# A new issue list for a fused attention and double feed-forward kernel: order, engine letters and buffer places

## The chip, the cores and the metric

The kernel runs on 1 core of one Trainium2 chip. The metric is device time in microseconds (us) of one execution, lower is better. The names of the engines are those of the profile: PE (TensorE, matmuls), PEld (TensorE's weight loads, which overlap PE), DVE (VectorE), ACT (ScalarE), POOL (GpSimd) and SP (SyncE, which here issues every DMA).

## The reference

Four batches of eight heads (576 positions, 64 wide) go through causal attention that is mixed with a read from a memory matrix, then through two feed-forward layers (512 to 2048 to 512) with different non-linearities.

```python
scores = where(causal, -1e9, scale * q @ k.T);  a = softmax(scores);  local = a @ v
q_p = where(q > 0, q, exp(q) - 1) + 1
mem_out = (q_p @ M_prev) / (q_p @ z_prev + 1e-6)
g = 1 / (1 + exp(-beta))
x = g * mem_out + (1 - g) * local          # heads side by side: 2304 x 512
h = x @ w_in;   g1 = where(h >= 1, h, where(h <= -1, 0, (h + 1)**2 / 4));  y = g1 @ w_out
h = y @ w_in2;  g2 = maximum(h, 0) + alpha * minimum(h, 0);                return g2 @ w_out2
```

## The kernel before

Every value that goes into a large matmul is split into a float16 head and a float16 rest, and each product is made of three float16 matmuls (head by head, head by rest, rest by head). The work is written section by section: `prepare` (sums and scales of a batch), `attend` (attention of a pair of heads), `Weights.groups` and `SumsIn.group` (weights arrive as float32 words and are scaled and split), `up1` and `down1` (first feed-forward layer, for each batch `b` and each of two halves of 288 tokens), `ffn2` (second layer, by a scheme with seven products in place of eight).

No section calls an engine. The class `Plan` (lines 86 to 136) records each operation with its number, 0 to 4286 in the order in which the sections write them. Many operations are recorded in more than one way (`either`, line 105): a scaling copy can be made by ACT, DVE or POOL (`copy`, line 225), the rest of a split by DVE in one instruction or by POOL in two (`rest`, line 243), a difference by DVE or POOL (`combine`, line 240), bits of a weight by DVE or ACT (`rest_of`, line 309). A group of matmuls under `plan.one()` is one operation, for example the 12 matmuls of 288 columns that give one block of `up1`.

Two tables written out by hand decide the rest. `ISSUE` (line 1259) lists the 4287 numbers in the order of issue, with a letter `a`, `v` or `g` (ACT, DVE, POOL) behind a number that has a choice; each engine, and SP with its DMAs, then takes its own instructions in that order. `PLACES` (line 1176) says for every tile of a name which of the buffers of this name it takes, as a string of digits. A tile that takes a buffer over waits until the tile before it there has been used for the last time. The instructions are all recorded in line 135, `fn(*args, **kw)`, so the profile shows L135 everywhere and is read by tiles.

Some names: `f` is the PSUM buffer (two of them, each for two blocks) of `up1`, `down1` and the last products; `d` and `u` are the steps of the first non-linearity (DVE clamps `f` into `d`, ACT squares it, DVE makes `u` out of `f` and `d`, which frees `f`); `g` holds the split result, `wt` and `wb` pass the weights through, `wa` holds w_in, `p` and `tt` are the softmax weights and their transpose, `s` and `px` are the smaller PSUM buffers (two each).

```python
    def run(self):
        engines = dict(a="act", v="dve", g="pool")
        order = ISSUE.split()
        ...
            for t in order:
                op = self.ops[int(t.rstrip("avg"))]
                eng = engines[t[-1]] if op.key else next(iter(op.ways))
                for fn, args, kw in op.ways[eng]:
                    fn(*args, **kw)
```

Of the kernel before, what the change touches and what calls it, by code (L numbers as in the profile page):

```python
# [1156 lines left out]
def _order():  # L1157
# [11 lines left out]
    for b in range(B):  # L1169
# [15 lines left out]
    "sb.qn": (640, "132040130124213041320423120431324014203114210420143042314034021324101340023123011243"),  # L1185
# [4 lines left out]
        "1010010110111001011110010110010101110010011010011010010101011010101010100101101010100101101010011001"  # L1190
        "1010100100011110010101101010101001101010011010010110100101010110010101011001011010100110101001011000"
        "011001110011000000100011101001100111110011101001110100001110011100",
    ),
    "tiny.arm": (1, "100010110"),
    "tiny.ard": (8, "0101"),
    "tiny.m3": (3, "0101"),
    "tiny.p2m1": (1, "01000101111001001001010101010110000000010101"),
    "tiny.p2e1": (1, "01001111000110011010001011010000010011011001"),
# [3 lines left out]
    "tiny.p2i3": (3, "0110"),  # L1202
# [4 lines left out]
    "sb.wt": (1024, "100101000011001101101101101101101101101100100110"),  # L1207
    "tiny.wmg": (1, "1001110001010101"),
    "tiny.ws": (1, "10011100001100111010101010100110"),
    "sb.x": (1152, "23011001011002130210321023103120321"),  # L1210
    "sb.vf": (1152, "1021021221021021021021012010"),
    "sb.qk": (1152, "101001011010101101010101"),
    "ps.px": (512, "10100101001011000111000001001100010011011001011100101101010001010101101010100011"),
    "tiny.mxt": (4, "32010121032313022310102301320113022303120112230231300122310231302103"),
    "tiny.sm": (4, "32010121032010322013132031320113022303120102231230312011302130021320"),
    "sb.e": (1152, "021201002121200102120121021020120120122001112020122001211022020101210212012"),
    "sb.p": (1280, "0010011001100110100101110001100011100011101010010101100010110100011001101010"),
    "sb.tt": (1280, "010101011101100010010110011001110001100010101001010110100111100001101000101010010101"),
    "ps.f": (
        1024,  # L1220
        "1010011001101011010010111010000101011010100100010011100101100101001100010110101001011110100110011010"
        "1001100101001011011010011101010010000010111011001100",
    ),
    "tiny.inv1": (8, "01010101"),
# [10 lines left out]
    "sb.g": (1152, "02133021420412043021410321034021324013240132410324"),  # L1235
    "sb.u": (
        576,
        "0101010110110001000111011010110001001011011100101010100100001111100101010101001001101011110000110110"
        "0101001110010011110100111001",
    ),  # L1240
    "sb.d": (576, "010010111011000111000110010100111001010101101010010101100000111101010101010110101010011010010101"),
    "tiny.wmx": (1, "0011001110100110"),
    "tiny.ysc": (4, "010101010101"),
    "sb.y": (288, "1110100100101001111010010101101010110011011011111010110010100010"),
# [8 lines left out]
    "tiny.p2s1": (1, "01001111"),  # L1253
    "tiny.p2i1": (1, "01000111"),
# [8 lines left out]
205 156 204 233 87v 160 231 840 33 161 169 170v 162 312 46 239a 173v 214 47 206 207 163 48 20 208a 164 209g 172 50  # L1263
210v 49 827 223v 15 211 1311 165 215 313 167a 174 129v 217 168v 18 212a 213 104 85 236v 238 216 315 235 240 120 218
237 495 171 241 219 220 122 314 21 221g 121 242 841 175 222v 462 842 243 123 166 107 244 124 245 246 224 463 125 248g
109 843 111 335a 108 249v 133 110 225a 19 320v 226 332v 268 331 126 134 266 128g 127a 135 136 142g 529 333 130 137 526
112 251v 113 852 51 115a 114g 52 334 116g 53 138 117 54 336 55 118a 197g 56 131a 139 59 119 57 188 58 141v 140a 132 60
189 349 190 191 317v 269 265 192 61 143 337 271 464 62 193 194 63 270 195g 273 278v 338 196g 272 502v 198 144a 274 176
65 64 304g 339 199a 145 340 341 342 275 344v 277a 200 276a 348 467a 279 66 591 345v 227a 836 148a 146a 828 177 316 346
247 350 319 318 560 853 178 321 834 179 322 180 147v 347 182g 149v 352 351 267 280a 181 323 229v 354 183v 353 829 324  # L1270
830 250 355 295 325 253 252 326 835 327 255 329g 328 860 356 256 297 296 357v 299 330v 257 481a 298 258 466 282 300
259 228v 470a 301 468 303a 302g 260 343 494 283 577a 262 261 359g 284 305 230v 469 263v 285 471 286 363 306a 291g 465
287 264v 631 472 307 365 501 288 358v 290v 498 360 289v 473 499v 292 361a 364 367 500 362 366 503 496 484a 393 474 837
376 475 394 368 372v 476 293v 504 478g 844 281 369 377 370a 378 505 371g 294 379 479v 380 373 628 385g 374v 483 480
485 548a 381 477 497 506 395 482 630 382 507 384a 508 383g 396 310v 397 486 308v 510g 386 309v 375 387a 402 511v 831
388 513v 512 832 403 398 594 515 514 487 389a 68 527 488 531a 390v 593 489 509 629 407 490 399 516v 492a 517 493v 406
518 558 592 401 491 530 405 519 404 456 408 534a 532 533 409 520 455 535 521 536 559 523 522 410 524g 632 666 457 391a
537 563a 421 411g 668 538 458 642g 604v 525v 833 420 412g 459 562 913 539 565 541 413 540 422 460g 845 564 423 414
461g 528 566a 424 542a 567 442 415 561 543g 311v 416 441 568 417 392v 434 418a 443 419v 444 435 425v 545a 445 426g 547
544 428 436 549 437 569 546 427 861 446g 570 438 550 447g 571 633 572 429 580a 448 574g 430 634 635 636 575v 595 637  # L1280
638 449 573 576 639 596 641g 431 598 640g 597 579 643 578 599 646 450 620g 644a 854 600 601 648 451 590 603g 647 581
667 649 439a 602g 400 582 645 651 708 440g 650 653 605 432v 652 583 551 658g 584 855 552 654 862 608 655 452 657g 606a
707 610 656g 661 609 856 453v 659 662a 857 611 660a 858 613 669 663 863 612 670 615 454g 859 722 705 614 553 607 706
723 664a 718g 724 864 616 725 617 665v 618a 619g 726 433g 621 727 728 623 585 622v 709 729 734g 865 846 624a 704 730
711 866 625 1085 731 710 713 554 712 732g 671 867 733a 714 586 715 626a 735 672 717g 847 737 673 716g 848 736v 684
680g 738a 849 719 675 685 850 674 686 627v 687 720a 676 739 696g 677 555 689 679a 678g 688 691 588g 851 681 690 910
868 721 869 682a 870 692 871 693 873 589v 874 694a 683 556a 875 697 876 872 695a 877 764 878 890 698a 879 880 887 888
881 882 889 883 699 891 885 892 914g 765 700a 893 587 884 915g 740v 911a 701 912v 995 743 702a 894 905 895 1086a 900
886 703v 2574 901 744 903 941 766 952g 942 931g 742 944 896 943 906g 767 945 953v 907v 996a 741v 1329 916 557v 768 745
1087v 750 919 1000 1750 923 918 908 920 899 1330 997v 746 922 1093 917 937a 946 947 1003 948v 1312 960 949v 747 909  # L1290
924 950v 806 749 1001g 961 921 1339 925 951v 963 932g 926 807 748 954 927g 929v 933g 962 1004g 898 964 751 938g 1005v
1002v 752 928v 808 975 934v 809 1751 930v 753 935v 965 810 936g 966 977 811a 792 902 939 1752 976 754 1340 969g 978
1341 904 955 979 1090 793 981 999 970v 756 1094g 980 998 982 812v 800 971g 967a 983 794 972g 1021a 968g 799 1753 795
940 1265 1027g 796 973 1095g 1006 801 757 1009 802 1010 1007 1028g 1008 1013 758 803 1022g 1014 1089 958a 1342 1011
1012 759 1754 797a 959v 1015 1759 1091v 798g 984 1016 1017a 1019a 771 985a 989v 987v 1023a 990v 760 1018v 804a 1347
# [207 lines left out]
```

## Time and profile before

| | us |
|---|---|
| median of 3 runs | 967.76 (967.29 to 969.53) |
| profiled execution | 971.3 |
| its span, first to last instruction | 969.5 |
| PE busy | 899.2 (93%), 8043 matmuls |
| PEld busy | 679.8 (70%) |
| DVE busy | 732.9 (76%), 1905 instructions |
| ACT busy | 520.1 (54%), 1109 instructions |
| POOL busy | 393.6 (41%), 487 instructions |
| DMA | 144.5 MB, 53.7% of the engines' span |

The profile page gives the span in 40 slices of some 24 us, each with a digit for the busy tenths. The view by stretches gives the same in us for stretches of one's choice, the view of waits says which instruction ended the idle time of an engine, and the timeline lists instructions in order of time. "Idle before" an instruction is the time in which its engine did nothing ahead of it.

### The profile page before, as it was taken

The numbers are of one execution on the slowest core, as the hardware profiler recorded it, in microseconds if no ns is written. First come the engines' busy times: TensorE is split into PE (matmuls) and PEld (weight loads), VectorE is DVE, ScalarE is ACT, GpSimd is POOL, SyncE is SP. The second block draws the span as 40 slices with busy tenths as digits, with TensorE's granted clock in tenths as the row PEclk, the third lists the DMA queues.
The fourth block names the chain that finished last, engine by engine and source line by source line (L and its number), as shares of the span: only waits on it lengthen the run. The fifth ranks groups of instructions, "written<-read, shape, count | busy, mean of one in ns | idle before, by whom it ended". The sixth has DMA issues, their size and how long they took to land. (4 is left out here: it accounts for less than half of the span.)

```text
span 969.5 us, 21105 instructions
## 1 busy us (share of the span) xinstructions
PE 899.2 (93%) x8043; PEld 679.8 (70%) x8043; DVE 732.9 (76%) x1905; ACT 520.1 (54%) x1109; POOL 393.6 (41%) x487
## 2 busy tenths in 40 slices
PE   1567999999999998998999999989999999999998
PEld 1345667777777766766677778767777777777776
DVE  5988898898888989979887688899767767464400
ACT  6988895687766757657765344466312212121100
POOL 3222673754647546466446252364322114121210
PEclk9968999999999999999999999999999999999999
DMA  8965334689848688368786436556433432331000
GB/s 284 346 212 193 99 121 145 121 182 183 191 113 172 126 168 178 123 178 195 166 188 191 130 134 220 191 174 221 136 126 105 154 93 81 99 101 46 25 25 26
DMA packets 157190, 144.52 MB, mean 149 GB/s; under 512 B 100000, under 2 KB 119968, under 8 KB 157088
## 3 DMA queue, kind: packets, MB, share of 16 engines
q1 hardware_dynamic: 157088, 143.17, 53.7%
q8 instruction: 63, 1.03, 0.5%
q14 instruction: 39, 0.32, 0.1%
HBM read 99.63 MB, written 16.78 MB: 120 GB/s over the span
## 5 line engine op out<-in xcount | busy, mean ns | idle before, releaser
L135 PEld LDWEIGHTS <-wb 128*128 128x128 f16 x3072 | 297.6, 98 | 86.2 <-issue 9.3
L135 PEld LDWEIGHTS <-wa 128*128 128x128 f16 x2880 | 279.6, 98 | 90.1 <-issue 17.9
L135 PE MATMUL f<-g,wb 128*128 128x288 f16 x2160 | 283.5, 287 | 3.2 <-DVE u L135 1.5
L135 PE MATMUL f<-x,wa 128*128 128x288 f16 x1536 | 201.1, 288 | 7.3 <-DVE u L135 6.5
L135 ACT ACTIVATE e<-e,mxt 128x192 f32<-128x192 f32 (+4 forms) x160 | 88.1, 551 | 32.2 <-DVE mxt L135 27.8
L135 PE MATMUL px<-x,wa 128*128 128x288 f16 x672 | 97.4, 286 | 2.0 <-DVE qn L135 2.0
L135 PE MATMUL s<-x,wa 128*128 128x288 f16 x672 | 97.8, 287 | 1.1 <-DVE qn L135 1.1
L135 ACT ACTIVATE y<-f,ysc 128x288 f32<-128x288 f32 x64 | 31.6, 496 | 119.1 <-PE f L135 101.0
L135 ACT ACTIVATE d<-d,bu,su 128x576 f32<-128x576 f32 x64 | 55.3, 864 | 52.8 <-DVE d L135 52.4
L135 POOL TENSOR_TENSOR g<-u,g 128x576 f16<-128x576 f32 x46 | 62.7, 1365 | 31.1 <-ACT g L135 14.1
L135 PE MATMUL s<-qk 64*128 64x288 f16 (+9 forms) x528 | 65.5, 322 | 5.8 <-DVE mxt L135 3.8
L135 DVE SCALAR_TENSOR_TENSOR qn<-qn,al 128x576 f32<-128x576 f32 x64 | 53.8, 852 | 13.5 <-ACT qn L135 13.1
L135 DVE TENSOR_SCALAR d<-f,lim 128x576 f32<-128x576 f32 x64 | 55.8, 872 | 10.1 <-PE f L135 9.7
L135 PE MATMUL px<-tt,vf 128*64 128x128 f16 (+3 forms) x1320 | 58.0, 236 | 4.0 <-ACT tt L135 2.6
L135 POOL TENSOR_SCALAR p<-e,sm 128x448 f16<-128x448 f32 (+9 forms) x52 | 31.4, 609 | 71.2 <-DVE sm L135 44.3
L135 DVE SCALAR_TENSOR_TENSOR u<-f,sd,d 128x576 f32<-128x576 f32 x64 | 52.1, 814 | 10.5 <-ACT d L135 9.2
L135 DVE CUSTOM_DVE_ANT_0 e<-s,mask,qs 128x192 f32<-128x192 f32 (+4 forms) x120 | 55.1, 482 | 4.8 <-PE s L135 4.6
L135 DVE SCALAR_TENSOR_TENSOR p<-e,sm,p 128x320 f16<-128x320 f32 (+4 forms) x89 | 51.9, 599 | 4.3 <-POOL p L135 2.0
L135 PE MATMUL f<-vf,wb 128*128 128x288 f16 x384 | 52.3, 286 | 0.0
L135 ACT ACTIVATE p<-e,sm 128x448 f16<-128x448 f32 (+8 forms) x80 | 43.1, 563 | 13.5 <-DVE sm L135 8.5
L135 PE MATMUL f<-e,wb 128*128 128x288 f16 x336 | 45.7, 286 | 0.0
L135 POOL TENSOR_TENSOR g<-qn,g 128x288 f16<-128x288 f32 x32 | 26.7, 845 | 42.7 <-ACT g L135 16.6
(249 smaller groups left out, 1398.9 us busy)
## 6 DMA issues: line engine op xcount, KB each, us to landing
wa<-w2i_d SPq DMA_DIRECT2D x32, 768.0 KB, 4.8
tmp<-in_qk SPq DMA_DIRECT2D x36, 288.0 KB, 3.3
wb<-in_w1i SPq DMA_DIRECT2D x16, 512.0 KB, 8.0
wt<-in_w2i SPq DMA_DIRECT2D x16, 512.0 KB, 4.2
w2i_d<-tmp SPq DMA_DIRECT2D x24, 256.0 KB, 2.6
x<-in_w1o SPq DMA_DIRECT2D x11, 512.0 KB, 3.9
qn<-in_qn SPq DMA_DIRECT2D x16, 320.0 KB, 4.0
tmp<-in_vc SPq DMA_DIRECT2D x16, 320.0 KB, 4.1
```

The costliest lines, as they stand in the source:

```text
L135: fn(*args, **kw)
```

## The change

Only the two tables change. The 4287 operations, their sections and their arithmetic stay. In `ISSUE` 4152 of the 4287 numbers stand in another place, most of them by few places. PE's 834 groups of matmuls keep their sequence but for small swaps: of the 558 groups that run before 675 us none moves by more than 11 places. SP's 426 DMAs move by 4.5 places on average. Of the 1388 operations with a choice of engine, 550 get another letter:

| from \ to | DVE | ACT | POOL |
|---|---|---|---|
| DVE | | 86 | 141 |
| ACT | 84 | | 65 |
| POOL | 95 | 79 | |

In `PLACES` the digits of most names change; the number and the size of the buffers do not. The diff, cut to its beginning and its kinds:

```diff
     "sb.tmp": (
         640,
-        "1110102011102220020000112122001212111000010211220021101220110021012102001210200102122112002010212121"
-        "0000201112021211202211022010121021021021",
+        "1200001210221210022020210212001220010202121012022100220202012120112011000212000112220021000212010121"
+        "0000210010200212022121101021102210102102",
     ),
...
-    "sb.wa": (2048, "012303213201320103210310132001231230"),
-    "sb.wb": (2048, "102313203120"),
+    "sb.wa": (2048, "012303123103120302310132101320313012"),
+    "sb.wb": (2048, "103212301230"),
...
 ISSUE = """
-1 72 2 1304 0 40 5 3 13 4 6 22 69 34 91 1305 1310 92v 1306 71 1307 93 41 1308 42 70 7 8 23 9 10 43 24 28 1309 11 44
-74a 151 73 35 25 234 36 75 89a 26 45 838 88 12 76 187 90 37 29 185 94 27 150 38 77a 95 184 30 78 16 39 79 153 31 839
-80 96 32 105 254a 97 152 81 98 201 100 99 82 158v 101a 83 186 84 106 86a 102v 232 17 203 202 157 155v 14 154 159 103
...
+1 22 3 5 34 0 2 1304 40 13 6 23 72 28 24 1305 70 1306 35 25 36 1307 71 26 1308 41 42 69 37 91 7 1310 27 38 187 29 153
+92a 43 77a 8 39 44 150 1309 88 9 30 93 76 151 89v 74a 90 73 78 14 94 75 45 79 231 95 31 80 152 1311 155a 10 96 32 173a
+81 97 201 82 16 98 158a 83 100 11 4 84 99 12 33 86g 101a 232 202 203 15 87v 827 204 236a 103 102v 157 104 154 184 159
...
```

Numbers 69 to 72 are the loads of the first group of w_in's words, 94 and 79 are ACT's squares of that group (its scale comes from them), 95 and 80 the matmuls that sum these squares.

## Rows read from the trace of the kernel before

**Rows 1.** The page: span, busy time of each engine, and PE's 40 slices.

```profile
span 969.5 us, 21105 instructions
...
PE 899.2 (93%) x8043; PEld 679.8 (70%) x8043; DVE 732.9 (76%) x1905; ACT 520.1 (54%) x1109; POOL 393.6 (41%) x487
...
PE   1567999999999998998999999989999999999998
```

**Rows 2.** Stretches: length, busy PE, PEld, DVE, ACT, POOL; clock, DMA share, GB/s.

```profile
0.00:125.00 125.00, 79.22 (x481) 53.12 (x482) 99.70 (x318) 102.49 (x210) 42.76 (x55) 0.88 0.68 226
125.00:350.00 225.00, 221.75 (x2298) 161.89 (x2298) 199.93 (x614) 161.01 (x384) 129.54 (x160) 1.00 0.68 149
350.00:510.00 160.00, 147.95 (x1580) 107.67 (x1577) 143.08 (x414) 110.98 (x245) 85.43 (x115) 1.00 0.74 173
510.00:640.00 130.00, 128.17 (x1083) 101.71 (x1081) 102.43 (x207) 60.38 (x100) 53.06 (x57) 1.00 0.52 170
640.00:675.00 35.00, 30.92 (x238) 23.50 (x237) 33.66 (x56) 24.09 (x46) 21.32 (x18) 0.95 0.61 207
675.00:969.50 294.50, 291.17 (x2376) 231.94 (x2374) 154.06 (x301) 61.19 (x129) 61.51 (x83) 1.00 0.27 87
```

**Rows 3.** Waits of PE, 0 to 125 us: total, times, longest.

```profile
PE s L135 <- ACT wa L135: 24.3, 4, 12.9
```

**Rows 4.** Waits of PE, 350 to 510 us.

```profile
PE f L135 <- DVE u L135: 5.4, 5, 1.8
PE s L135 <- DVE mxt L135: 2.7, 6, 1.8
...
PE px L135 <- DMA tt<-p: 0.7, 1, 0.7
```

**Rows 5.** Timeline, 371 to 377 us, of DVE, POOL and PE: start, us, instruction.

```profile
372.35 1.30 POOL L135 TENSOR_TENSOR p<-e,p 128x576 f16<-128x576 f32 x1
372.43 1.77 DVE L135 SCALAR_TENSOR_TENSOR wt<-wt,wt 128x512 int32<-128x512 int32 x1
...
374.86 0.81 DVE L135 SCALAR_TENSOR_TENSOR u<-f,sd,d 128x576 f32<-128x576 f32 x1
...
375.73 1.51 PE L135 MATMUL f<-x,wa 128*128 128x288 f16 x11 [1.75 <-DVE u L135]
```

**Rows 6.** Groups by shape: busy us and mean ns of one, then idle before.

```profile
L135 POOL TENSOR_TENSOR g<-u,g 128x576 f16<-128x576 f32 x46 | 62.7, 1365 | 31.1 <-ACT g L135 14.1 <-DVE p2s L135 7.6 <-DVE g L135 4.8
...
L135 DVE TENSOR_TENSOR g<-u,g 128x576 f16<-128x576 f32 x18 | 14.6, 817 | 0.8 <-ACT g L135 0.7
...
L135 ACT ACTIVATE u<-s,sa 128x288 f32<-128x288 f32 x17 | 8.4, 494 | 4.2 <-PE s L135 4.2
```

**Rows 7.** Instructions by tile (wt, then d): duration min/median/max in ns.

```profile
L135 DVE SCALAR_TENSOR_TENSOR wt<-wt,wt x16: 680/684/1771, 238.7 to 561.9; 128x512 int32<-128x512 int32 x16
L135 DVE SCALAR_TENSOR_TENSOR wb<-wt,ws,wb x13: 1273/1284/2426, 79.5 to 685.9; 128x1024 f16<-128x1024 f32 x13
...
L135 DVE TENSOR_SCALAR d<-f,lim x64: 847/874/879, 92.7 to 582.2; 128x576 f32<-128x576 f32 x64
```

**Rows 8.** Timelines: SP's loads and ACT's squares at the start.

```profile
0.74 0.39 SPq L135 DMA_DIRECT2D wb<-in_w1i  x1
...
3.54 0.43 SPq L135 DMA_DIRECT2D wb<-in_w1i  x1
...
8.49 0.65 SPq L135 DMA_DIRECT2D qn<-in_qn  x1
...
15.55 0.75 ACT L135 ACTIVATE wb<-wb,half 128x512 int32<-128x512 uint16 x1
...
17.95 1.04 ACT L135 ACTIVATE wa<-wt 128x1024 bf16<-128x1024 f32 x1
```

**Rows 9.** Timeline at the end, and up1's matmuls of the first 125 us by duration.

```profile
L135 PE MATMUL f<-x,wa x192: 283/286/448, 88.5 to 119.4; 128*128 128x288 f16 x192
...
966.26 0.50 ACT L135 ACTIVATE y<-f,ysc 128x288 f32<-128x288 f32 x1 [5.38 <-PE f L135]
```

More of the change, by code (lines that the diff above doesn't have):

```diff
@@ L1210 @@
[L1210 to L1216, printed above, removed]
@@ L1217 @@
-    "sb.p": (1280, "0010011001100110100101110001100011100011101010010101100010110100011001101010"),
-    "sb.tt": (1280, "010101011101100010010110011001110001100010101001010110100111100001101000101010010101"),
+    "tiny.ws": (1, "01011100001100111010101010101010"),
+    "sb.x": (1152, "32011010001013021302130213012031023"),
+    "sb.vf": (1152, "0101120212012012012012021020"),
+    "sb.qk": (1152, "101001011010010010101010"),
+    "ps.px": (512, "10101101110100110111000000101111100011010001011010100010010101101011101110101011"),
@@ L1219 @@
+    "tiny.mxt": (4, "32010121032313022310102301320113022303121002231230311022301230312013"),
+    "tiny.sm": (4, "32010121032312033210103201230112033202131013320321203100213321103201"),
+    "sb.e": (1152, "021201002112200102120121020121021021002112220101200112022102121010201202102"),
+    "sb.p": (1280, "1001010110010100100101110001100011101001101010010101010010100111100101001001"),
+    "sb.tt": (1280, "100101001110010101101001100101010010001110010110101010011100011110110001101001101010"),
     "ps.f": (
@@ L1220 @@
         1024,
[L1221 to L1222 removed]
+        "1001010001011011010010110011000110001010110111000011100110001100011100010110101011001001010101100101"
+        "0110101010110100010101010101101001111100001101101101",
     ),
[L1224 removed]
+    "tiny.inv1": (8, "01010110"),
     "tiny.bd": (1, "01010101"),
@@ L1252 @@
     "tiny.ym1": (1, "0101"),
-    "tiny.p2s1": (1, "01001111"),
-    "tiny.p2i1": (1, "01000111"),
+    "tiny.p2s1": (1, "01001110"),
+    "tiny.p2i1": (1, "01001010"),
     "tiny.amx": (1, "0"),
@@ L1265 @@
[L1265 to L1274, printed above, removed]
@@ new lines @@
+1212 1213 1214 1131v 1215 1155 1326 1134 1316 1274 1216 1157 1327 1156 1217 1220a 1158 1218v 1083a 1272 1275 1222g
+1160 1317 1219g 1159 1162 1328 1186 1161 1223g 1221v 1120 1313 1187 1163 1290 1819 1164 1224 1189 1165a 1167g 1190
+1188 1169a 1084v 1193 1170g 1135 1271 1194 1168v 1291 1140 1191 1166v 1192 1280 1195 1142 1171 1196 1207g 1201a 1197v
+1276 1205a 1141 1198g 1199a 1203a 1200v 1136a 1202g 1208v 1143 1225 1204v 1206v 1144 1137v 1230 1209 1138a 1281 1232
+1145 1234 1146 1231 1151g 1282 1147v 1233 1152g 1292 1314 769 1148g 1331 1139v 1283 1277 1149a 1278 1279 1235 1241g
@@ new lines @@
+1559 1739 1713v 1562a 1560g 1712v 1930 1563v 1715 1955 1561g 1931 2423 1923 897 1716 1742a 1925 1717 1963 2422 1924
+1740a 1745v 1566 1743v 1718 1741g 2430 2424 1933 2425 2429 1719 2426 1956 1720 2436 2427g 1721 2431 2611a 1957 2432
+2437 2428v 1964 1958 2433 1953 2438 1724a 2415 1960 2434a 1746 1965 1722a 1725v 2416 2439 1966 1959 2610 2440 1567
+1961 2417 2435g 2441a 2401 1726a 1967 2418 1727g 2612 2402 1984 2419 2613 1723v 2420a 2614 1985 1728 2403 1934 2394
+1986 2615 2404 1987 2616 1989 2617 1568a 1990 2619 2395 2618 1991 1988 1992 2026 2620g 2442g 2621g 2622g 2421g 2627a
@@ new lines @@
+2921 3163a 2973 2810a 2962 2922 3173 2974a 2811g 2923 2963 2924 3157g 2812 2935 2964 3199 2912 3143 2965 2925v 2934
+2975v 2926g 2966 3175 2936 3225 2948 2571 3155v 2937 3164v 3010 2967a 2949 2938 3016 3176 2939v 3251 2950 3200 3202
+2940g 2919 3112 2951 3226 2813g 2952 3113 2814v 2953a 3158v 3015 3179 2954v 3167a 2976 3174 3171g 3144 3105 3145 3146
+3147 3148 3149 3150 3151 3017 3106 3180a 2968v 3027 3107 2980 3172v 3169a 3203v 3108 2981 2572 2982 3170v 3201 2978
+3109 2986 3177v 3114 3111 3110 3011 3178 2815 3204 2987 3181 2988 2989 2990 2991 3183 3168v 3207 2992v 3119 3182v
@@ new lines @@
+3590 3534v 3536v 3591 3531v 3506 3413 3483v 3501 3393 3504v 3502g 3505v 3089g 3594 3542 3547 3597 3394 3598v 3503g
+3545 3509g 3414 3546a 3548 3553 3395 3415 3482v 3554g 3555g 3549 3510g 3566 3550 3556g 3601 3103v 3567a 3551 3507g
+3599 3552v 3615 3508g 3616 3396 3558 3484g 3399 3559v 3397 3602 3560g 3600 3557g 3565 3603 3568 3605 3400 3604a 3824
+3823 3564 3618 3726 3569 3619a 3416 3617 3570v 3608v 3606g 3607g 3571 3620 3609g 3644 3572a 3438 3561a 3405 3645a 3575
+3573 3406 3574 3579 3407 3610 3576 3611a 3582a 3612g 3621 3408 3622v 3727v 3583v 3401 3409 3613v 3580v 3614v 3410
@@ new lines @@
+3949a 3951g 3908a 4020v 3698 3821g 3950v 3952g 3909 3699 3910v 3700 3913 3911 4023a 3914 4034 3701 4025g 3912 3915
+3917 4060 4021g 3916a 4109 4027a 3702 4008 3692 3822g 4110 3920v 4028v 4059 4022v 3693 3918v 4009 4061v 3919v 4063
+4035v 4062 4033 3922 3694 4029v 3925a 4064a 3923v 4024v 4037 3926v 3695 3924v 3709 3696 3893v 4084 4036 4026v 3710
+4030v 3921v 4039 4067 4040a 4038a 4065 3711 4066v 4068 4073 4086 4069 4076g 4087a 4041 4070 4043 4042 4071 4089 4072v
+4044 3712 4090v 4047 4085 3713 4045 3714 4088 4161 4078 4093 4046a 4213 4010 4091 4079a 4048a 3977 4092v 4162 4094
@@ new lines @@
+4052 4115 4099 4055a 3959 4050a 4053g 4102a 4056v 4116a 4054g 4112 4080v 4051g 4095 4113v 4100g 4111 4081v 4077g 3960
+4114 4082g 4103g 4096 4117 4097 4118a 4074a 3961 4098v 4135 4104 4119 4107v 4105g 4049v 4121 4106g 3978 4108v 4101g
+4120 4125 4163 4128v 4138 4129v 4122 3979 4126v 4127v 3962 4137 3963 4123 3964 3980 4124a 4188 4130 3953 4131a 4133v
+3981 4134v 4139a 4132g 3982 4136 4164 4187 4167 3708 4165v 3954 4166 4168a 4140 4169 3971 4170a 3955 4173 3956 4174
+4141 3957 4143 4142a 4145 4175 4171 4176a 3989 4172 3972 3973 3974 4193 3975 4144a 3965 3976 4194v 4146 4151 3966
@@ new lines @@
+4152g 4153v 3967 4177 4180v 4182 4147 4183a 3990 4184v 4148 4075v 3968 3991 3969 4178a 3970 4179g 4149 4185g 3992
+4186g 4150v 4156 4190 3993 4216 3994 4191a 4214 4219 4217v 3983 4220a 4154a 4155g 4197 4215 4189 3984 4192 3995 3996
+3997 4195 3998 4196v 4198 4203 3985 3999 4159a 4204v 4000 4218 4206v 4223 4207g 4199 4160g 3986 4200 4157g 4201 3987
+4221 3988 4202a 3958 4208 4251 4211v 4209g 4212v 4252 4158g 4222v 4224 4210g 4225 4205g 4257 4226 4229 4227 4232v
+4230g 4253 4231g 4228a 4234 4233g 4258 4235g 4237g 4236g 4259 4238g 4181g 4254 4260 4255 4281 4261 4262 4282 4283 4284
@@ L1446 @@
+4239 4285 4286 4240 4269 4270 4271 4272 4241 4273 4274 4242 4245 4243 4244 4275 4276 4246 4247 4248 4277 4249 4250
+4278 4263 4279 4280 4256 4264 4265 4266 4267 4268
 """
```

350 lines of the change are left out of this document (161 added, 189 removed).

## The prediction

> **What bounds the kernel now.** I read the page first, then the stretches, then the waits of PE in the stretches where it is idle. On the page [rows 1] PE is busy for 899.2 of 969.5 us, and its slices show where it is not: in the first four, then a little in the middle (two digits of 8). The stretches [rows 2] give that in us. From 0 to 125 us PE is idle for 125 - 79.2 = 45.8 us; from 125 to 350 for 3.2; from 350 to 510 for 12.1; from 510 to 640 for 1.8; from 640 to 675 for 4.1; and from 675 to the end for 3.3. So PE sets the time from about 125 us on, and there are 45.8 us to win or lose at the start and 3.2 + 12.1 + 1.8 + 4.1 = 21.2 us in the middle. The last 3.3 us are no stall: the last copy out of PSUM starts at 966.26, behind PE's last matmul [rows 9], and its store follows. Behind 675 us nothing can be won, since 2376 matmuls in 291.2 us are one in 122.5 ns at a clock of 1.00, 2.4 GHz, and 288 columns at 2.4 GHz take 120.
>
> What holds PE at the start: it waits 24.3 us for ACT's `wa` (the squares from which a weight group gets its scale), more than half of its idle time there [rows 3]. ACT is busy for 102.5 of these 125 us, DVE for 99.7 [rows 2]; both are nearly full, and the chains run through both.
>
> What holds PE in the middle: of 350 to 510 us the two largest waits are for DVE, 5.4 us for `u` and 2.7 for `mxt` [rows 4]. DVE is busy for 143.1 of 160 us there, and for 199.9 of 225 before [rows 2]. One such wait stands in the timeline [rows 5]: DVE is at a weight instruction of 1.77 us, then `u` starts at 374.86, and only then PE, idle for 1.75 us, gets its `f` buffer back. So DVE, in its own queue, runs late by a few us, and PE has only two `f` buffers to bridge that.
>
> **The change, part by part.** Nothing is added to PE, and its sequence hardly moves, so its work stays as it is. What can change is when its inputs come.
>
> *Letters.* 227 operations leave DVE and 179 come to it. I counted them by the stretch in which the trace runs them, and priced each by its own duration on the engine it leaves and the mean of its shape on the engine it goes to. Two kinds stand in [rows 6]: the rest `g<-u,g` takes 0.82 us on DVE and 1.37 on POOL, a copy `u<-s,sa` 0.49 on ACT. For DVE this gives:
> 0 to 125 us: 26 leave, 17 come, -3.2 us;
> 125 to 350: 60 and 42, -9.4;
> 350 to 510: 35 and 26, -5.4;
> 510 to 675: 33 and 34, +1.7;
> later: 73 and 60, -6.2 (PE waits for nothing there, so worth nothing).
> To 510 us that is 36 instructions fewer, 18.0 us, half a us each. POOL gets +2.4, +17.9, -0.6, -1.3 and +13.5 us in the same stretches, ACT +2.4, -0.6, +8.9, +1.2 and -4.4.
>
> *Order.* It works the same way. Ahead of the `u` of [rows 5] DVE has 836 operations in the old list and 805 in the new one, while PE's place is the same but for a few groups. So the relief is ahead of the stalls, not behind them.
>
> *What POOL's time costs DVE.* The same timeline shows why DVE was late just there [rows 5]: the `wt` instruction took 1.77 us beside a POOL instruction of 1.30, and its median is 0.68 [rows 7]. Instructions of DVE that read PSUM do not show this: `d<-f,lim` takes 0.847 to 0.879, 64 times [rows 7]. How much more the added POOL time costs, the trace does not show directly. One bound is 0. The other is that each added us of POOL stops DVE for one us: 2.4 + 17.9 - 0.6 = 19.7 us by 510, more than the 18.0 of relief. From rows: `wt<-wt,wt` has a mean of 0.865 (16 take 13.8 us) against a minimum of 0.680, `g<-u,g` on DVE 0.817; stretches of 10 to 25% where both inputs come from SBUF. POOL is busy for 215 of the 385 us from 125 to 510 [rows 2], and 17.3 more is 8%; 8% of a stretch of some 20% on half of DVE's 343 us is under 3 us. I take 2.
>
> The Trainium skill, "SBUF — State Buffer", section "Who interferes with whom", says that a DVE instruction with two SBUF inputs and a GpSimd instruction that reads SBUF take an exclusive lock, and the one that comes second is blocked for the whole instruction. The trace agrees [rows 5] (1.77 is near 0.68 plus most of 1.30). By that rule alone the price would lie at its upper bound and the time at 971 us; that is the first rival.
>
> *The middle, summed.* DVE is relieved by 18 - 2 = 16 us by 510. PE can win back no more than it lost. Of the 12.1 us of 350 to 510 I take two thirds, -8: most waits for DVE go, those like the 0.7 us for a DMA [rows 4] stay. Of the 3.2 before, a third, -1. Of 1.8 + 4.1 behind, a third, -2: the wait near 650 us is also a chain of its own, and once PE is earlier there DVE has only some us more in hand. What is late next is POOL, with slower rests (1.37 for 0.82) that `down1` and the attention wait for; but it is busy half of the time, and ACT with +8.9 from 350 to 510, at 111 of 160 us. For such new stalls I put +1, between 0 and +6 (half of the gain). Sum of the middle: -10, between -21 and +2.
>
> *The start.* ACT has 14 instructions ahead of the first square (17.95 us) and 16 in the new list; at 0.75 us [rows 8] the first sum of squares comes 1.5 us later. On SP, the four loads of this first group stand in places 1, 7, 9 and 10 of the queue, now 7, 9, 10 and 11: the last one is issued at 8.49 rather than before it, and the first at 3.54, the seventh issue, rather than at 0.74 [rows 8]. Against that ACT gets other loads to work on first. Over 125 us ACT gets +2.4 us and DVE -3.2. I take +2 for the start, between -3 (DVE's relief is felt in full) and +7 (the late weights and ACT's extra time add up, and some of up1's first matmuls fall to the lower clock). The trace shows a granted clock of 0.88 over these 125 us, and up1's matmuls at 0.286 and, at the lower level, 0.448 us [rows 9].
>
> *Sum*: -10 + 2 = -8 us on the profiled 971.3 (span 969.5 and 1.8 around it), 963. That execution is 3.5 us above the median of the runs, so against the median 967.76 the forecast is 959.8 us.
>
> **The rivals.**
> *POOL takes it back (slower).* Place: DVE between 125 and 510 us. Price: with a share r of the added 19.7 us blocking DVE, the relief is 18.0 - 19.7 r. The middle's gain of 10 shrinks in proportion, 10 x (18.0 - 19.7 r) / 16, and the start's +2 outweighs it from r = 0.75 on. At r = 1 the stalls grow by 1 and the start adds 2: 971. For it speaks the blocked `wt` [rows 5]; against it that the blocked instructions are few: the median of `wt` is 0.684 against a minimum of 0.680 and that of `wb` 1.284 against 1.273, so most pass untouched [rows 7].
> *A late start (slower).* ACT and the first loads are late by 5 us, and PE is thinner in up1's first blocks, which stay at the lower level, 1.2 GHz. Those 192 matmuls then cost up to 0.448 - 0.286 = 0.16 us more each, up to 31 us in all; a quarter of them is 8. With the middle's -10 that is 5 + 8 - 10 = +3, 971; it decides from about 30 matmuls at the lower level on. The clock of 0.88 speaks for it, the full one from 125 us on [rows 2] against it.
> *All of DVE's waits go.* PE runs dense from 125 to 675 us: -19 of the 21.2, with a start of 0: 949. For it: 16 us of relief against 12.1 of idle time. Against it: 640 to 675 is a chain of its own.
> *It does nothing.* The middle's waits are short chains from PE through DVE to PE, and the new order has others in their place: -1, with the start +1: 968. DVE's own idle time there (17 of 160 us) speaks for it, as it was not full.
>
> **How the numbers follow.** The forecast (-13 to -4) gets 0.50, all waits gone 0.17, nothing 0.13, POOL 0.10, the late start 0.10. About 0.2%, 1.9 us, is what a measurement of this kernel can tell from no change. Faster by more: 0.50 + 0.17 + 0.03 of "nothing" = 0.70. Within: 0.10 of "nothing" and 0.02 of POOL = 0.12. Slower: 0.08 + 0.10 = 0.18. The range runs from 949 (all waits gone) to 971 (the two slower ones at their price). The forecast's own range is 955 to 964.
>
> **What would show it.** Right: DVE's busy time before 510 us falls by some 16 us, PE's idle time from 350 to 510 from 12.1 to about 4, PE's wait for `u` there from 5.4 to under 2, the same 45 to 49 us of idle time before 125 us, and 675 us of now are reached some 8 us earlier. Wrong: PE's idle time at the start grows by over 5 us, or DVE's busy time hardly falls although it has fewer instructions (then POOL blocks it), or waits of PE for POOL or ACT stand where those for DVE were.

## The result and the profile after

The new list takes 956.97 us (median of four runs, 956.56 to 958.13) where the old one, run beside it, took 968.64 (967.29 to 973.17): a ratio of 0.9873 [0.9839, 0.9908] (in brackets, here and below, the 95% interval), 11.7 us less. A second measurement of the same kernel gave 0.9894 [0.9862, 0.9925]. The profiled execution took 956.56 us, with a span of 954.8. Its page, to be held against [rows 1]:

```profile
span 954.8 us, 21134 instructions
...
PE 895.7 (94%) x8043; PEld 680.6 (71%) x8043; DVE 717.7 (75%) x1857; ACT 526.9 (55%) x1125; POOL 420.2 (44%) x533
...
PE   1578999999999999999999999989999999999998
```

DVE is busy for 15.2 us less, POOL for 26.6 more, PE for 3.5 less. The slices show where PE gained: in the third and fourth slices, and in the two of the middle that showed an 8 and are full now. The stretches, with the columns of [rows 2]:

```profile
0.00:125.00 125.00, 84.44 (x528) 57.84 (x528) 105.34 (x332) 110.56 (x225) 48.35 (x66) 0.85 0.69 235
125.00:350.00 225.00, 221.24 (x2318) 162.10 (x2317) 199.91 (x590) 157.27 (x374) 141.81 (x193) 1.00 0.68 153
350.00:510.00 160.00, 153.98 (x1645) 113.87 (x1645) 145.14 (x412) 124.45 (x267) 94.07 (x114) 1.00 0.78 180
...
```

Stretches of time hold other work once a kernel runs earlier (528 matmuls instead of 481 in the first), so I also took the start of the n-th matmul in both traces. It comes 1.2 us earlier at n = 200 (80.1 us in the old trace), 7.3 at n = 480 (124.9 us), 7.0 at n = 3000 (370.0), 14.8 at n = 4000 (477.3), 16.0 at n = 5600 (666.5) and 14.7 at the last one. In the second trace of the new list it is 8.6 us at n = 480, 5.5 at n = 3000 and 12.1 at n = 4000. So the gain has two places: 7 to 9 us before 125 us, and 7 to 8 us between 370 and 477.

The same measure shows what became of DVE's work. Up to n = 4400, which the old list starts at 515.6 us and the new one at 499.9, DVE was busy for 447.3 us and is now busy for 442.2 (443.7 in the second trace): 5.1 or 3.6 us less.

The next two fences are PE's waits from 0 to 125 us [rows 3] and from 350 to 510 us [rows 4].

```profile
PE s L135 <- ACT wa L135: 22.9, 4, 11.8
PE s L135 <- DVE amx L135: 5.5, 1, 5.5
PE s L135 <- DVE mxt L135: 3.3, 4, 1.7
```

```profile
PE s L135 <- ACT wt L135: 3.4, 2, 1.8
PE px L135 <- DMA tt<-p: 0.7, 1, 0.7
PE f L135 <- DVE u L135: 0.6, 2, 0.3
PE s L135 <- DVE mxt L135: 0.5, 1, 0.5
```

In the middle the wait for `u` fell from 5.4 to 0.6 us and that for `mxt` from 2.7 to 0.5; a new one for ACT's `wt` stands first, with 3.4. At the start no single wait explains the 7 us. What differs most there is ACT: its waits from 0 to 125 us, old list first.

```profile
ACT tmp L135 <- DMA tmp<-in_vc: 3.3, 2, 3.1
...
ACT tmp L135 <- DMA qn<-in_qn: 2.5, 2, 1.9
ACT gt L135 <- DMA gt<-in_beta: 2.2, 1, 2.2
ACT wt L135 <- DMA wb<-in_w1i: 2.2, 1, 2.2
ACT x L135 <- DMA x<-in_w1o: 1.4, 1, 1.4
...
ACT wb L135 <- DMA wb<-in_w1i: 1.1, 1, 1.1
```

```profile
ACT wt L135 <- DMA wb<-in_w1i: 3.0, 2, 2.6
ACT tmp L135 <- DMA qn<-in_qn: 2.4, 2, 1.9
...
ACT x L135 <- DMA x<-in_w1o: 1.2, 2, 0.9
```

ACT waited 12.7 us for loads and now waits 6.6; it does 110.6 us of work before 125 us instead of 102.5.

### The profile page after: what moved, and what is told of

Read it like the earlier page. It is cut to its first block, busy times and chain, and to the rows that moved or that the text cites. A ratio compares the mean times of both kernels' runs of the same rounds, so it can differ in the third digit from the quotient of the medians.

```text
span 954.8 us, 21134 instructions
## 1 busy us (share of the span) xinstructions
PE 895.7 (94%) x8043; PEld 680.6 (71%) x8043; DVE 717.7 (75%) x1857; ACT 526.9 (55%) x1125; POOL 420.2 (44%) x533
## 4 chain that ended last, share of the span: by engine, by line
PE 51%; DVE 6%; DMA 5%; ACT 3%; issue 1%; SPq 0%; POOL 0%; DVEq 0%; ACTq 0%; POOLq 0%
PE f L135 33%; PE s L135 9%; PE px L135 9%; DMA tt<-p 2%; DMA wt<-in_w2i 1%; DMA tmp<-in_qk 1%; DVE wt L135 1%; ACT p L135 1%; ACT tmp L135 1%; ACT wt L135 1%; DVE e L135 1%; DMA tmp<-in_vc 1%; DVE p L135 1%; DVE qn L135 0%; DVE u L135 0%
## 5 line engine op out<-in xcount | busy, mean ns | idle before, releaser
L135 PE MATMUL f<-x,wa 128*128 128x288 f16 x1536 | 196.7, 286 | 0.9 <-DVE u L135 0.3
L135 ACT ACTIVATE y<-f,ysc 128x288 f32<-128x288 f32 x64 | 31.7, 495 | 140.7 <-PE f L135 113.3
L135 ACT ACTIVATE e<-e,mxt 128x64 f32<-128x64 f32 (+4 forms) x160 | 88.0, 551 | 17.9 <-DVE mxt L135 13.7
L135 POOL TENSOR_TENSOR g<-u,g 128x576 f16<-128x576 f32 x48 | 65.4, 1368 | 28.0 <-DVE g L135 14.2
L135 ACT ACTIVATE d<-d,bu,su 128x576 f32<-128x576 f32 x64 | 55.2, 863 | 40.6 <-DVE d L135 40.3
L135 PE MATMUL s<-qk 64*128 64x288 f16 (+9 forms) x528 | 62.2, 323 | 3.3 <-DVE mxt L135 2.9
L135 DVE SCALAR_TENSOR_TENSOR u<-f,sd,d 128x576 f32<-128x576 f32 x64 | 52.0, 813 | 15.3 <-ACT d L135 12.1
L135 DVE CUSTOM_DVE_ANT_0 e<-s,mask,qs 128x64 f32<-128x64 f32 (+4 forms) x120 | 54.8, 481 | 4.7 <-PE s L135 4.7
L135 ACT ACTIVATE p<-e,sm 128x448 f16<-128x448 f32 (+8 forms) x88 | 49.1, 584 | 13.7 <-DVE sm L135 7.8
L135 POOL TENSOR_TENSOR g<-qn,g 128x288 f16<-128x288 f32 x29 | 24.1, 837 | 70.0 <-DVE g L135 36.2
L135 DVE SCALAR_TENSOR_TENSOR p<-e,sm,p 128x192 f16<-128x192 f32 (+4 forms) x77 | 45.0, 601 | 2.7 <-ACT p L135 2.2
L135 POOL TENSOR_SCALAR p<-e,sm 128x64 f16<-128x64 f32 (+9 forms) x49 | 26.7, 553 | 43.3 <-DVE sm L135 20.3
## 6 DMA issues: line engine op xcount, KB each, us to landing
wb<-in_w1i SPq DMA_DIRECT2D x16, 512.0 KB, 7.6
wt<-in_w2i SPq DMA_DIRECT2D x16, 512.0 KB, 3.9
x<-in_w1o SPq DMA_DIRECT2D x11, 512.0 KB, 4.3
```

## The experiments

Times of different sessions are compared by their ratios to the old list, which ran beside each.

**Letters alone, order alone.** The first takes the old list and its buffer places with the new letters, the second the new list and places with the old letters (the first numbers of each list):

```diff
-1 72 2 1304 0 40 5 3 13 4 6 22 69 34 91 1305 1310 92v 1306
+1 72 2 1304 0 40 5 3 13 4 6 22 69 34 91 1305 1310 92a 1306
```

```diff
-1 72 2 1304 0 40 5 3 13 4 6 22 69 34 91 1305 1310 92v 1306
+1 22 3 5 34 0 2 1304 40 13 6 23 72 28 24 1305 70 1306 35 25
```

> The old order and the old buffer places with the new engine letters alone. Theory (the middle was won because DVE has 36 instructions, 18 us, less to do before 510 us; the start was won by the order): the middle keeps most of its gain and the start gives nothing, so 6 to 10 us less than the kernel before, 958 to 962. Rival (the order won both): within 2 us of the kernel before. Rival (letters fit only the order they were found with): slower by 2 us or more.

> The new order and places with the old engine letters. Theory (letters win the middle, order the start): the start's 6 to 7 us are kept and the middle's are mostly lost, 959 to 963. Rival (the order won both): 956 to 958, as fast as the changed kernel. Rival (order and letters only work together): no faster than 966.

Measured: 1.0446 [1.0403, 1.0488] for the letters alone, 43 us slower, and 1.0257 [1.0217, 1.0298] for the order alone, 25 us slower. PE's waits over the whole span, letters alone and then order alone (the old list has 8.0 us for `u` and 7.7 for `mxt` over its span):

```profile
PE f L135 <- DVE u L135: 20.0, 20, 2.9
PE s L135 <- DVE mxt L135: 13.4, 19, 2.6
```

```profile
PE f L135 <- DVE u L135: 14.0, 18, 1.6
PE s L135 <- DVE mxt L135: 9.8, 17, 2.6
```

The letters alone leave DVE the 1857 instructions of the new list, and yet it is busy for 741.1 us, 8.2 more than in the old list, and late twice as often. So what the letters save in the new list isn't a property of the letters. Order and letters, taken whole, are worth something only together. The buffer places go with the order in both runs and weren't tried by themselves.

**The start alone, the rest alone.** Two spliced lists, with buffer places worked out anew: the first 648 numbers of the old list in the new order with the new letters, then the old list; and the first 644 numbers of the new list in the old order with the old letters, then the new list.

```diff
-ISSUE = old list
+ISSUE = (the old list's first 648 numbers, in the new order, new letters) + (the old list from 649 on)
```

```diff
-ISSUE = new list
+ISSUE = (the new list's first 644 numbers, in the old order, old letters) + (the new list from 645 on)
```

> The first 648 operations of the old list (to about 124 us) in the new order and with the new letters, all later ones as before. Theory (the start's gain is a gain of its own, 6 to 7 us, which PE carries to the end): 960 to 963. Rival (an earlier start is lost again, since DVE in the middle is late anyway): 965 to 968.

> The counterpart: the start as before, everything behind it in the new order and with the new letters. Theory (the middle's gain stands alone): 7 to 10 us less than before, 958 to 961. Rival (the middle gains only when it starts early): 963 to 967. If the two halves add up, the gains of this one and of its counterpart sum to that of the whole change, some 12 us.

Measured: 0.9897 [0.9855, 0.9939] with the new start, 10.0 us faster; 0.9945 [0.9919, 0.9971] with the old start and the new rest, 5.3 us faster. In the trace of the first the 480th matmul starts 9.1 us earlier than in the old list's, and 6.5 of that last to the end. In the second it starts 0.3 later, 4.2 us are lost by n = 1500, just behind the seam, and 6.6 are won from there to n = 4400. Both parts pay. The start's gain is the larger of the two, but the intervals overlap; the gains sum to 15.3 us where the whole change has 11.7, which the intervals allow.

**One late load at the start.** In the old trace ACT stands still for 3.1 us up to 65.8 us, for a load that a square of batch 1 wants, with the square that PE waits for queued behind it. That square and the load that reuses its buffer are moved behind the urgent one:

```diff
-... 252 326 835 327 ... 329g 328 860 356 ... 256 297
+... 252 326 327 ... 329g 328 356 ... 256 835 860 297
```

> The old list with one instruction moved: the square of a batch 1 tile on ACT (and the load that takes its buffer over) goes from just ahead of the 768-column square of the w1i group, which the first scores wait for, to just behind it. In the old trace ACT stands 3.1 us idle at 62.7 to 65.8 us for that load and the urgent square lies behind it. Theory (the start's gain comes from urgent ACT work no longer queued behind instructions whose load is late): the 4.36 us stall of PE at 63.3 us falls to about 1.5 us, and 2 to 3 us of it last to the end, about 965 to 967 us, ratio 0.997. Rival (something else is late there as well, so PE stalls at another place): the stall shrinks but the end does not move, ratio 0.999 to 1.001.

Measured: 0.9991 [0.9970, 1.0013]. Lines of PE's timeline from 60 to 72 us, first of the old list, then with the square moved:

```profile
67.66 1.01 PE L135 MATMUL s<-wa,ones 128*128 128x256 bf16 x4 [4.36 <-ACT wa L135]
...
71.13 1.12 PE L135 MATMUL f<-ident,p 128*128 128x128 f32 x4 [0.94 <-POOL p L135]
```

```profile
67.20 1.01 PE L135 MATMUL s<-wa,ones 128*128 128x256 bf16 x4 [1.60 <-DVE p L135]
...
71.83 0.47 PE L135 MATMUL f<-ident,p 128*128 128x128 f32 x1 [2.07 <-POOL p L135]
```

The 4.36 us stall for ACT's `wa` became one of 1.60 for DVE's `p`, but the next one, for POOL's `p`, grew from 0.94 to 2.07 us. This fits the rival: several chains are late there at once, and removing one of them shows the next. The 0.997 of the theory lies at the edge of the interval.

**More work on DVE, more on POOL.** Instructions on constants that nothing waits for, spread over the middle: 36 on DVE in the new list and in the old one, and 40 on POOL in the new one.

```diff
+    for _ in range(36):
+        V.tensor_reduce(out=padr, in_=ident.unsqueeze(1).to_broadcast([P, 3, P]), axis=AX, op=ALU.max)
```

```diff
+    for _ in range(40):
+        G.tensor_tensor(out=padr, in0=ident, in1=ones, op=ALU.subtract)
```

> The new list with 36 extra reductions of 384 constants on DVE, each some 0.47 us by the nearest rows (17 us in all), that nothing waits for, spread evenly over 118 to 500 us. Leaves nothing out of the result. Theory A (what DVE has to do is what bounds the middle, so the 16 us that the letters take off it are the gain): the middle loses about what it won, 8 to 12 us, 965 to 969 us. Theory B (the new list has slack on DVE and the gain comes from order and letters fitting together, so that few instructions arrive late): 0 to 4 us, 957 to 961 us. DVE is busy for about 144 of the 160 us between 350 and 510 us, which speaks for A there.

> The old list with the same 36 extra reductions on DVE, spread over 125 to 510 us. Theory A (DVE's load bounds the middle of the old list): 17 us more of DVE cost at least 8 to 12 us, 976 to 980 us, and more than in the new list, since DVE is fuller. Theory B (the old list loses its time at single instructions that come late, not through load): 0 to 5 us, 968 to 973 us. That the old list loses clearly more than the new one would show that the new list's worth lies in its slack.

> The new list with 40 extra subtractions of two 128-column tiles on POOL, some 0.45 to 0.53 us each (18 to 21 us in all), that nothing waits for, spread over 118 to 500 us. It prices what the prediction's rival feared of POOL. If POOL's reads of two operands hold DVE up one for one: DVE's blocked time grows by 10 us or more and the end by 5 to 10 us, 962 to 967 us. If as the prediction took it (an eighth of POOL's time): 2 us of DVE, 957 to 960 us. If POOL's own queue bounds the new list (POOL is busy 142 of 225 us between 125 and 350 us): waits of PE or DVE for POOL's results grow, over 5 us.

Measured: the new list with more for DVE 0.9918 [0.9881, 0.9954], the old list with the same 1.0105 [1.0074, 1.0136], the new list with more for POOL 0.9915 [0.9886, 0.9944]. The 36 instructions took 19.5 us in both traces. They cost the old list 10.2 us, and the new list 2.3 or 4.4, counted from either of its two measurements. So an added us on DVE costs the old list half a us and the new one an eighth to a quarter; the intervals of the new list's three ratios overlap, so its part is rough. POOL's 40 took 22.4 us, between 0.448 and 1.111 each, so part of that is time in which POOL itself was held up; at the shortest they would be 17.9. The engines' line of that run's page:

```profile
PE 888.5 (93%) x8043; PEld 675.3 (70%) x8043; DVE 725.4 (76%) x1857; ACT 526.9 (55%) x1125; POOL 440.2 (46%) x573
```

With the same 1857 instructions DVE is busy for 7.7 us more than in the new list's first trace (6.5 more than in its second): about a third of POOL's added time. The kernel lost 2.0 to 4.1 us. PE's and DVE's waits for POOL grew from 13.8 to 15.6 us in sum, less than the 5 us that would have pointed to POOL's own queue. The prediction took 2 us for 17.3, a ninth; its first rival took the whole: both miss.

**DVE made lighter, nothing else.** Where query, key and value tiles are split, the 31 DVE instructions that form the remainder copy the high half instead, so the kernel leaves the remainders out; order, letters and places stay. This is done in the old list, then in the new one. The new list itself ran beside them.

```diff
-            if e is V:
+            if e is V and light:
+                V.tensor_copy(out, hi)
+            elif e is V:
                 V.scalar_tensor_tensor(out=out, in0=src, scalar=scale, in1=hi, op0=ALU.mult, op1=ALU.subtract)
...
-            rest(vf[:, 0:5, 1], raw, s3[:, 0:1], vf[:, 0:5, 0], (G, V))
+            rest(vf[:, 0:5, 1], raw, s3[:, 0:1], vf[:, 0:5, 0], (G, V), light=True)
...
-                rest(qt[:, 1, i], raw, q_s[b][:, i : i + 1], qt[:, 0, i], (V, G))
+                rest(qt[:, 1, i], raw, q_s[b][:, i : i + 1], qt[:, 0, i], (V, G), light=True)
```

> The old list, order, letters and places untouched, with DVE's work made lighter where it splits the query, key and value tiles: its 31 two-operand instructions (20 of 0.92 us, 11 of 0.98 us, all between 125 and 510 us) copy the high half instead of forming the remainder, so the low halves hold no remainders (that part of the computation is left out). They wait for the same producer as before. A copy of 16-bit values is estimated at 0.2 to 0.4 us from the 0.30 to 0.36 us of a cast of 288 columns, so DVE is relieved of some 17 to 23 us, about the 16 us that the prediction credited to the new letters. Theory A (DVE's time bounds the middle of the old list, as the prediction had it and as the 10.2 us for 19.5 us of extra work suggest): the middle gains 8 to 12 us, 958 to 963 us. Theory B (what counts is that list and letters fit, not DVE's total): 0 to 4 us, 966 to 971 us.

> The same lightening of DVE in the new list (31 instructions, 29.7 us in its trace, to some 7 to 12 us; the low halves hold no remainders, that part of the computation is left out). If DVE's time still bounded the new list's middle, as it cost 4.4 us to add 19.5 us: 3 to 5 us, 953 to 955 us. If the new list has what it can get there (PE idle for 3.8 us between 125 and 350 us and 6.0 us between 350 and 510 us, the latter mostly for ACT): 0 to 2 us, 956 to 958 us.

> The new list once more, unchanged, as the base on this chip for the two runs beside it and for a second trace: 0.986 to 0.989 of the time before. Before 125 us its trace should show again that the 480th matmul starts 6 to 10 us earlier than in the old list's; if it is within 4 us, the start's gain was a matter of the single execution.

Measured: the lighter old list 0.9975 [0.9951, 0.9999], the lighter new list 0.9884 [0.9857, 0.9911], the new list 0.9894. So the new list gains 1.0 us by it, which is within the interval of none. These are DVE's copies in the lighter old list (columns as in [rows 6]), and then that run's page:

```profile
L135 DVE COPY qk<-qk 128x576 f16<-128x576 f16 x20 | 8.3, 423 | 4.6 <-ACT qk L135 3.7 <-POOL qk L135 0.9
L135 DVE COPY vf<-vf 128x640 f16<-128x640 f16 x11 | 4.6, 418 | 0.0
```

```profile
PE 898.6 (93%) x8043; PEld 681.3 (71%) x8043; DVE 717.6 (74%) x1905; ACT 520.7 (54%) x1109; POOL 386.6 (40%) x487
```

DVE is busy for 717.6 us, what the new list has (717.7). Up to n = 4400 it is busy for 432.7, 14.6 less than in the old list and nearly three times the 5.1 that the new list saves there, though at other instructions. The gain is 2.4 us, between 0.1 and 4.7 by the interval, where theory A had 8 to 12. PE's waits from 350 to 510 us in it, against [rows 4]:

```profile
PE f L135 <- DVE u L135: 6.5, 6, 2.0
PE s L135 <- DVE mxt L135: 3.2, 5, 1.9
```

They didn't fall; the window holds one more of the stalls listed below (at 507.9 us here, at 512.0 in the old trace), and counted stall by stall they are 7.0 us against 7.1. The timeline shows why, at the very stall of [rows 5], which comes 1.4 us earlier here:

```profile
369.59 0.88 DVE L135 TENSOR_SCALAR d<-f,lim 128x576 f32<-128x576 f32 x1
...
370.38 0.44 DVE L135 TENSOR_REDUCE ym<-y 128x1 f32<-128x288 f32 x1
...
370.74 0.33 DVE L135 TENSOR_TENSOR p<-qn,p 128x128 f16<-128x128 f32 x1
371.00 0.68 DVE L135 SCALAR_TENSOR_TENSOR wt<-wt,wt 128x512 int32<-128x512 int32 x1
...
371.02 1.79 POOL L135 TENSOR_TENSOR p<-e,p 128x576 f16<-128x576 f32 x1
...
372.41 0.87 ACT L135 ACTIVATE d<-d,bu,su 128x576 f32<-128x576 f32 x1
372.56 0.94 DVE L135 SCALAR_TENSOR_TENSOR qn<-qn,tmp 128x640 f32<-128x640 f32 x1 [0.88 <-ACT tmp L135]
...
373.43 0.81 DVE L135 SCALAR_TENSOR_TENSOR u<-f,sd,d 128x576 f32<-128x576 f32 x1
```

Between the clamp `d` and the `u` of the same block the old list has four DVE instructions: `ym`, `p`, `wt` and `qn`. Here `wt` starts 0.02 us ahead of POOL's `p`, not 0.08 us behind it, and takes 0.68 us instead of the 1.77 of [rows 5]; this time it is `p` that is longer, 1.79 us for 1.30. The shorter `wt` doesn't help: `qn` then waits 0.88 us for ACT's `tmp`, and ACT's own instruction on `d` comes only behind that `tmp`, 1.94 us after DVE has left `d`. From the start of `d` on DVE to the start of `u` it takes 3.84 us; in the old trace 3.79, from 371.07 to 374.86. The same block in the new list:

```profile
364.22 0.87 DVE L135 TENSOR_SCALAR d<-f,lim 128x576 f32<-128x576 f32 x1
...
365.01 0.15 DVE L135 TENSOR_REDUCE ym<-ym 128x1 f32<-128x8 f32 x1
365.12 0.87 ACT L135 ACTIVATE d<-d,bu,su 128x576 f32<-128x576 f32 x1 [0.40 <-DVE d L135]
...
366.02 0.82 DVE L135 SCALAR_TENSOR_TENSOR u<-f,sd,d 128x576 f32<-128x576 f32 x1 [0.87 <-ACT d L135]
```

One small instruction stands between them, ACT takes `d` at once, and `u` starts 1.80 us after `d`. DVE stands idle for 0.87 us for it, and PE doesn't wait.

The stalls are tied to places in the list. In the old trace PE stands for more than half a us at six groups of matmuls between 375 and 512 us until a `u` frees their `f` buffer: 1.75, 0.98, 1.00, 0.73, 1.26 and 1.37 us, 7.1 in all. (The profile puts the 0.73 down to `w2i_inv`, the small DVE instruction just behind that `u`.) Matched group by group, all six stand again in the old list with the square moved, with the new start and with the new letters alone, all six in the lighter list (1.97, 0.97, 1.00, 0.68, 1.02 and 1.33), and five with more work on DVE. In the five traces of the new list from start to end none of the six appears but for one of 0.75 in the run with more on POOL. In the new order with the old letters one of them is left, 1.57 us, though that list stalls at other groups. So the order takes these six away, and DVE's total doesn't.

What the order does is not the same at each. Take the time from PE's last matmul into an `f` buffer to the end of the `u` that frees it. For the stall of 1.75 us it was 4.64 us and is 2.77, for that of 1.26 it was 5.52 and is 3.38 (`d` starts 0.33 us after the buffer is full, not 2.00). These two, 3.0 of the 7.1 us, went with what stands on DVE and ACT. For the stall of 0.98 it was 2.92 us and is 4.25, longer, and yet PE no longer waits, because its own groups stand in another order. PE in the old list and then in the new one:

```profile
398.41 1.63 PE L135 MATMUL f<-g,wb 128*128 128x288 f16 x12 [0.36 <-DVE u L135]
401.02 2.24 PE L135 MATMUL f<-g,wb 128*128 128x288 f16 x17 [0.98 <-DVE u L135]
```

```profile
390.29 6.05 PE L135 MATMUL f<-g,wb 128*128 128x288 f16 x48
```

The old list turns to the second of the two `f` buffers after 12 matmuls of `down1`, the new one after 36. The stalls of 1.00 and 0.73 go mainly in the same way: there the old list puts a block of a third tile ahead of the two blocks of the second, and the new one fills tile after tile (at the 1.00 the chain also shrinks, from 3.47 to 2.93 us). The stall of 1.37 has only changed its name. Its chain takes 4.16 us for 4.37, and PE stands 1.54 us two groups earlier, for ACT's `wt`. Again the old list and then the new one:

```profile
512.00 1.88 PE L135 MATMUL f<-x,wa 128*128 128x288 f16 x14 [1.37 <-DVE u L135]
```

```profile
493.57 0.60 PE L135 MATMUL s<-wt,ones 128*128 128x256 bf16 x4 [1.54 <-ACT wt L135]
```

The new list has one more stall of its own, at 439.8 us, of 0.9 to 2.2 us in its five traces, for ACT's `wt` or DVE's `mxt`.

**The loads of the start.** The new list with its first 40 loads in the old list's order among themselves; no other engine's order or letter changes.

```diff
-1 22 3 5 34 0 2 1304 40 13 6 23 72 28 24 1305 70 1306
+1 72 3 5 1304 0 2 40 13 6 22 23 69 34 24 1305 71 1306
```

> The new list, every compute engine's order and letters kept, with the first 40 loads (issued up to 38.8 us in its trace) in the old list's order among themselves; one buffer place differs. Theory (the start's 7 us come from the loads: in the old trace ACT waits 12.7 us for loads before 125 us, in the new one 6.6 us): PE's start loses 4 to 7 us, 961 to 964 us. Rival 1, the prediction's own step (the old order brings the first weights sooner, so the new order of the loads costs time): 0 to 3 us faster, 954 to 957 us. Rival 2 (the start's gain lies in the compute engines' order): within 1 us, 956 to 958 us.

Measured: 1.0129 [1.0099, 1.0158], and 980.78 us against 958.74 for the new list beside it: 22.0 us lost. ACT's waits from 0 to 125 us:

```profile
ACT tmp L135 <- DMA qn<-in_qn: 9.0, 2, 8.3
ACT wb L135 <- DMA wb<-in_w1i: 7.5, 3, 5.0
ACT x L135 <- DMA x<-in_w1o: 3.4, 2, 3.0
ACT tmp L135 <- DMA tmp<-in_vc: 3.2, 1, 3.2
ACT tmp L135 <- DMA tmp<-in_qk: 2.8, 1, 2.8
```

ACT waits 25.9 us for loads where the new list has 8.1 in its second trace, and the 200th matmul comes 20.5 us later than there; at the end 19.8 are left. The loss is larger than the theory's 4 to 7: ACT waits far longer here than the 12.7 us that it waits in the old list with the same order of loads, so these loads fit the new queue of ACT worse than the old one. The run shows what the new order of loads is worth to this list, not that the loads alone would have won 7 us in the old one; the old compute order with the new loads wasn't tried.

## Why the prediction was right, and where it wasn't

The direction, the forecast and the range hold: 959.8 us was forecast, 956.97 measured, and the case was the likeliest. But the sum came out through two terms that both missed, in opposite directions: some -8 us at the start for +2, and some -5 in the middle for -10. That the forecast came within 2.8 us is luck in this sense.

*The start, +2 us between -3 and +7: wrong.* In five traces with the old start the 480th matmul starts at 120.5 to 125.2 us, in six with the new start at 113.3 to 117.6; the means differ by 8.2 us, and already by 5.0 at the 120th matmul, near 55 us. The failed step is the pricing of the start by counts and places: 16 instructions instead of 14 ahead of the first square, so "the first sum of squares comes 1.5 us later", and the four weight loads further back. In the new list both squares of the first group stand back to back on ACT:

```profile
17.77 1.99 ACT L135 ACTIVATE wa<-wt 128x1024 bf16<-128x1024 f32 x2
```

The first starts at 17.77 us against 17.95 [rows 8], the second at 18.72 against 20.59 (17.9 to 18.7 in the six traces, 19.7 to 20.6 in the five). The step asked when the weights are issued, and not what each in-order queue has at its head meanwhile. Putting the weights first again cost the new list 22.0 us. What makes up the 8 us beyond these 2 stays open: ACT's waits for loads before 125 us are 5.7 to 8.1 us in the six traces and 8.8 to 12.7 in the five, some 3 us apart in the mean, and removing one such wait in the old list gained nothing that shows. PE's idle time before 125 us is 40.6 us, not the 45 to 49 given as the sign of being right.

*The middle, -10: the right sign, about half the size, and another cause.* From n = 480 to n = 4400 three traces of the old list's middle that carry no added or lightened work take 390.7, 386.6 and 393.4 us, three of the new list's 382.3, 386.9 and 385.3: the means are 5 us apart, and one pair at a time gives anything from none to 11. The spliced list that has only the new rest gained 5.3 in all. The part that repeats best lies between n = 3000 and n = 4000, where five of the six stalls lie: 105.9 to 108.0 us with the old middle, 99.4 to 101.6 with the new one, and 106.0 in the lighter old list.

Two steps failed. The first is "DVE is relieved by 18 - 2 = 16 us by 510". Up to the same matmul DVE is busy for only 5.1 or 3.6 us less. The count was right: of the operations ahead of n = 4400 those that leave DVE took 60.3 us there and those that come take 41.3. But the 1022 that stay took 456.2 us and now take 467.7 (sums of durations, which overlap a little): the 2 us set against the relief came to 11.5. POOL's added time alone isn't the reason, since with the new order and the old letters the same operations take 468.0 us, with POOL busy for 400.5 us in the whole span, 6.9 more than in the old list. The second step is from DVE's total to PE's stalls, "PE can win back no more than it lost". The old list with 14.6 us of real relief gained 2.4 us, with the waits for `u` as before; the new letters in the old order lost 43. What took the stalls away is the order: at two of the six what stands ahead of and between `d` and `u` on DVE and ACT, at three mainly PE's own groups, and at one nothing was won. The prediction put PE's part at nothing, "its sequence hardly moves, so its work stays as it is"; 414 of the 558 groups before 675 us stand in another place, 1.7 places on average, and with two `f` buffers that is enough.

DVE's time isn't free (19.5 us more of it cost the old list 10.2), but losing by more work and gaining by less aren't the same slope: more work makes further places late, less of it doesn't move a late place that waits for ACT or for PE's own order. The lighter run relieves DVE at other instructions than the letters do; it tests the total, not each place.

*The signs.* PE's wait for `u` from 350 to 510 us fell to 0.6 (forecast under 2), as it would have with either cause, so it couldn't prove the one given. PE's idle time there fell from 12.1 to 6.0, and 8.0 in the second trace (forecast about 4). DVE's busy time was to fall by some 16 us and fell by 5.1 or 3.6; that it "hardly falls" was named as a sign of being wrong, and so were waits of PE for ACT in place of those for DVE, of which `wt` is one. So the signs spoke against the account, while the time agreed with it.

*POOL's price, 2 us of DVE for 17 to 20 us of POOL: too low.* The added reads cost DVE a third of their time. The rule of the Trainium skill that the prediction weighed, in "SBUF — State Buffer", section "Who interferes with whom", would make it nearly all of it if every read met a two-input instruction of DVE and came first; the measured 6.5 to 7.7 us for 22.4 lie between. By that third, POOL's 17.9 us more between 125 and 350 us cost some 6 us of DVE, an estimate from this run. It didn't decide the time, because the stalls don't follow DVE's sum.

*The late start and the lost clock* didn't come: the granted clock before 125 us is 0.85 in the first trace and 0.89 in the second, against 0.88 [rows 2], with the gain in both. The slow matmuls of [rows 9] belong to one execution: 16 of `up1`'s first 192 took 0.39 to 0.45 us in the old list's trace, most of them from 99 to 102.5 us at a granted clock of 0.51, the lower level; in the other ten traces counted above it is none to two.

## What to carry to other kernels

With in-order queues and shallow buffers, look at what stands on each engine ahead of a short chain and between its first and its last instruction, at what those in between wait for, and at how much other work the waiting engine has until it needs the buffer; an engine's busy total says little about a stall. A few places in the waiting engine's own order can be worth as much as a shorter chain. Order, engine choice and load order belong together: with one of the three taken from the other list, this kernel ran 22 to 43 us slower than the list that was altered. And a sign that two causes would both give isn't a test of either: make the suspected cost alone smaller, and see whether the stall goes.

## What was not expected of the hardware

The 36 added DVE instructions took 19.5 us in the new list, but DVE's busy time rose by only 13.4 (717.7 to 731.1), in the old list by 17.9; the others got shorter by the rest, and why is open. The time that DVE's instructions take above the tenth percentile of their shape is some 65 us in the new list's trace and in the old one's, although POOL is busy for 27 us more, and some 87 with the new letters in the old order: how often the two meet seems to depend on the list as much as on POOL's time. At one place the two traces shown above have the pair in either order: where POOL's `p` started 0.08 us first, DVE's `wt` took 1.77 us; where `wt` started 0.02 us first, it took 0.68 and `p` took 1.79 instead of 1.30. That was read from traces and not tried by itself. A copy of 576 16-bit values on DVE took 345 to 423 ns on average, at the upper end of the 0.2 to 0.4 us estimated from casts.
